# Rows turned on TensorE, and an angle's multiply-add moved to ScalarE, in the lead-in of a long-convolution kernel

## The chip, the cores and the metric

The kernel runs on one core of a Trainium2 chip. The time is device microseconds of one execution; the profile is one further execution, recorded by the hardware profiler. Engines are written as the profile writes them: PE (TensorE), DVE (VectorE), ACT (ScalarE), POOL (GpSimd), SP (SyncE, which issues most transfers).

## What is computed

Shapes: 2048 positions, 640 channels, MLP width 1728, all bfloat16. Cut to what matters here:

```python
mod = silu(c) @ w_mod                       # six vectors of 640: sa, ca, ga, sb, cb, gb
h = layernorm(x) * (1 + ca) + sa
# long convolution
k_shift = sum over t of k shifted by t * shift_k[:, t]     # 4 taps, per channel
kv = k_shift * v
y = irfft(rfft(kv, 4096) * rfft(ssm_k, 4096))[:2048] + kv * ssm_D
x = x + ga * (h * y)
h = layernorm(x) * (1 + cb) + sb
x = x + gb * mlp_block(h)                   # two GELU stages, four weight matrices
```

`ssm_D`, `c` and `shift_k` are small: 640, 640 and 640 x 4 numbers. Since y + kv * D is a convolution whose filter has D added to its first tap, the kernel adds D to column 0 of `ssm_k` before the transform.

## The kernel before

The FFTs are matrix products. Channels lie on 128 partitions in five blocks, b = 0 to 4. Each block of the filter is loaded (`sT`, a 512 KB transfer each), gets D added to its first column (L444), and is rearranged by a 32x32 transposition on DVE (L394, `to_slots`). Stage 1 of the transform (`stage1`) multiplies a block by the table F1bd: four matmuls of 256 columns (L407) per group, and one eviction of 1024 columns on ACT (L207) or DVE (L209). There are twenty such groups for the filter. Stage 2 (`stage2_half`, L427) needs all of them and a second table, `Gs` in region RG. Meanwhile the first blocks of k go through the shift filter (L463), a product with diagonal matrices made by L355 out of the shift coefficients.

All tables are computed in the kernel. An angle is an integer ramp (iota on POOL), multiplied by a per-partition number with an offset added, reduced modulo the table's length, and put through the ACT function Sin:

- F1bd: `angles` with 32 columns. DVE does the multiply-add (L292) and a bitwise AND (L293), twice each; ACT two sines (L321); POOL spreads the result into block-diagonal form (L332, L333).
- `Gs`, kb = 0, the first large table: the same with 512 columns, and a negated copy of the sines (L348, here on DVE).
- `Gs`, kb = 1: `angles_pool`, which reduces by rounding (L306 multiply-add, L308 rounding, L310 difference, each twice, on POOL, or DVE for one L306), then ACT sines (L316) and a negated copy on POOL (L348). The other half of RG is copied there by DMA (L353, L354).
- Later tables of 64 columns, and one in RK.

The per-partition numbers (`s32`, `s64`, `s32o`, `s64t`, `offc`) come from a block of small DVE instructions, L263 to L279, called the column setup below.

`Dcol`, `c_col` and `skT` hold D, c and the shift coefficients with the channel on the partition. Their transfers read one element of 2 bytes (8 bytes for shift_k) per partition and block: 640 pieces each. D is the first transfer on SP's queue, shift_k comes after four filter blocks, c much later (at 38.83 us).

Every piece of work is a task with a number, given to `add` in the order of the source. What runs where and in which order is written out by hand in a string, ORDER: `66D` is task 66 on DVE, `88P:0` is task 88 on PE with its PSUM result in slot 0 of four. A is ACT, G is POOL, S is SP. The engines take their tasks in the string's order and wait for each other by semaphores. The string begins

```python
0S 2S 19G 18D 50G 20D 21G 23D 22D 25A 4S 3S 1S 6S 27G 29D 36G 37G 28D 5S 8S 9S 11S 68G 10S
69D 24A 26G 88P:0 72G 73D 31A 30A 32D 38G 66D 89A 84P:1 85A 67D 90P:2 91A 86P:3 87D 39G 40A
```

0S is the load of D; 1S to 5S the filter blocks; 6S shift_k; 18D a few constants; 20D the column setup; 22D, 23D and 24A, 25A the F1 angles and sines; 26G F1bd; 28D to 31A the same for kb = 0 and 32D its negation; 68G, 72G and 66D the D additions of blocks 1, 3 and 0, and 69D, 73D and 67D their transpositions; 88P and 89A the first group of stage 1 with its eviction.

Of the kernel before, what the change touches and what calls it, by code (L numbers as in the profile page):

```python
# [8 lines left out]
BF = mybir.dt.bfloat16  # L9
F32 = mybir.dt.float32  # L10
I32 = mybir.dt.int32
ACT = mybir.ActivationFunctionType
# [14 lines left out]
0S 2S 19G 18D 50G 20D 21G 23D 22D 25A 4S 3S 1S 6S 27G 29D 36G 37G 28D 5S 8S 9S 11S 68G 10S 69D 24A 26G 88P:0 72G 73D 31A 30A 32D 38G 66D 89A 84P:1 85A  # L27
67D 90P:2 91A 86P:3 87D 39G 40A 102P:0 103A 100P:1 76P:2 70G 104P:0 41D 49G 101A 77A 42G 43G 105A 106P:3 107A 44A 45G 33S 47S 46S 71D 34S 12S 35S 48S
184S 181S 183S 182S 13S 14S 116P:1 92P:2 98P:0 74D 75D 117D 7S 99A 118P:3 119D 114P:0 15S 112P:1 113D 93A 110P:2 16S 115A 111A 96P:3 97A 94P:0 95D
82P:2 83A 80P:1 81A 78P:3 108P:0 51D 109A 52D 54A 56G 57D 53A 122P:2 79D 155P:1 156A 153P:0 154A 151P:3 152A 123D 157P:2 136D 120P:1 121D 173P:0 158A  # L30
55G 174A 171P:3 172A 177P:2 178D 175P:1 176A 161P:0 162D 141P:3 142A 167P:2 168D 147P:1 148A 58G 59G 163P:0 164D 165P:3 166A 137P:2 138A 145P:1 146A
230D 17S 149P:0 150A 190D 188D 126P:3 127D 139P:2 140A 60A 143P:1 199S 144A 124P:0 125D 179P:2 180A 187D 169P:3 170A 234P:1 235A 244P:2 159P:0 160A
128P:3 231D 242P:1 243A 245A 130P:0 61G 62G 186D 63G 64A 238P:1 239A 129D 131D 232D 248P:2 65G 196S 249A 246P:3 247A 185D 189G 191A 252P:0 202S 253A
134P:1 135D 132P:2 133D 236P:3 240P:1 237A 260P:0 261A 233D 250P:2 251A 241D 423D 200P:3 201A 258P:0 259D 319G 208S 192G 268P:2 269A 318S 197P:3 205S
198A 266P:1 267A 272P:2 273D 270P:3 271A 203P:0 284P:1 285A 292P:2 211S 204D 278P:3 279A 417D 276P:0 277A 342S 293D 426D 209P:1 210D 294P:2 295D 226S
290P:3 222G 291A 280P:1 281D 229G 227S 264P:0 274P:2 275D 343G 223G 265A 256P:3 262P:1 420D 206P:0 207D 257A 225G 254P:2 255D 282P:3 263A 286P:0
288P:1 287D 224G 312P:2 220S 283A 289A 212P:3 321D 320D 218G 213D 313A 328D 304P:0 305A 308P:1 316P:2 317A 217S 216G 302P:0 219S 214G 418D 228S 298P:2
215S 324P:3 325D 309A 221G 327G 326S 329D 322P:1 303A 336D 306P:0 299A 421D 323A 310P:2 296P:3 307A 334S 335G 337D 350S 297A 311A 300P:1 330P:0 301A
351G 332P:3 344D 345D 331A 314P:2 333A 315A 359G 340P:1 341A 338P:0 352D 348P:3 349A 353D 346P:2 358S 347A 360D 361D 354P:1 367G 339A 356P:3 368D 366S
369D 355A 364P:2 357A 375G 362P:0 376D 372P:1 374S 377D 401S 193A 363A 382S 370P:3 373A 384D 383G 385D 380P:0 378P:1 365A 392D 390S 391G 393D 422D  # L40
419D 424D 402P:2 427D 194D 403D 371A 388P:3 381A 379A 407S 389A 428D 386P:0 387A 416G 425D 396P:1 397A 394P:3 395A 398S 399P:0 400D 432P:12 429A 430D
434D 433A 489D 502A 510D 195G 413S 490D 491A 511D 530D 408P:3 513D 404S 405P:0 406A 531D 409A 512A 440S 492G 494D 475P:12 476A 477A 515D 532A 462P:03
463A 410S 411P:1 493G 495D 514G 435S 533D 534G 496A 497D 498G 441G 535D 464A 516D 536D 518D 499D 412A 517A 469P:20 537A 471A 519G 500P:3 538D 539G
414P:1 465G 470A 558D 449S 501D 520D 521P:3 436S 415A 507P:0 522A 443S 559D 560A 540D 541P:2 437S 542A 466P:13 431D 561D 562D 563A 564D 508A 546P:2
467D 468A 547A 548P:1 565G 448S 570D 528P:0 571D 566D 572D 567D 549A 573A 446S 568D 505P:3 506A 569A 574G 575G 447S 509G 529A 503D 523D 504D 621D 622D
472P:21 473A 526P:3 527A 623A 579D 580P:0 581A 576D 439S 543A 524D 577P:2 525D 624D 578D 625D 444S 438S 550P:3 627D 480S 551D 481S 626A 590P:0 591A
445S 482S 552A 588P:2 589A 595P:3 459D 628G 633D 629D 634D 553G 630D 631D 632A 635D 637D 636A 479S 554G 555D 556P:0 557A 592P:2 486S 596D 597A 638G
641A 639D 478S 488G 610P:3 612P:0 611A 593D 608P:2 606P:3 544D 594A 598D 613A 599G 474D 460A 603D 600D 601P:1 604P:0 609A 457D 607A 442S 454A 602A
640S 642S 651P:2 649P:3 461G 650A 450D 487S 652A 485S 605D 673P:0 667P:1 451D 545D 668A 674A 452G 582D 583D 484S 689D 690D 456A 458G 584D 585D 656P:3
692D 693D 653P:2 483S 614P:1 654D 655A 657D 694A 615D 659G 658A 671P:0 695D 660G 664D 665P:2 691A 661D 662P:3 663D 453D 669P:1 696G 701A 702D 703D  # L50
666A 735P:3 455G 672A 670A 697D 698D 699D 705G 737P:2 736A 739P:0 733P:1 616D 704A 643D 644D 645D 700A 738A 706G 709A 675P:32 710S 586D 587D 740A 755D
756D 757A 646A 707D 708S 758D 759D 717P:0 714D 761G 760A 762G 734A 763A 767D 777A 768D 711A 769D 719P:1 764D 780D 676P 718A 720A 721P:0 724P:1 647D
712D 765D 766A 677D 678D 770A 680S 771G 772G 683D 741P:32 648D 773D 774S 722D 775A 776S 785P:0 725D 726A 783P:1 713D 723A 824D 617S 825D 742P 821D
822D 827D 679S 681S 826A 743D 682S 727G 728G 731D 732S 823A 784A 828G 829A 786A 787P:3 729D 730S 833D 834D 835D 830D 831D 832A 837D 684D 685S 836A
620S 838G 790P:1 788D 789A 839D 840S 799P:0 791D 805P:3 806A 781D 841D 715D 716D 881D 749D 793G 792A 882D 842S 883A 803P:1 804A 794G 795A 796S 845P:2
846A 797D 778D 779D 884D 843P:3 844A 885D 887D 800A 801P:1 802A 618S 847P:2 848D 782D 941D 850P:3 851D 852A 886A 849A 619S 687S 798S 865P:0 866A
859P:1 860A 863P:2 807P:30 861P:1 744D 750D 753S 942D 944D 745S 853D 854G 855A 888G 893A 943A 752S 857A 889D 864A 945G 890D 856S 808P 858S 809D 891D
946A 947D 948D 950D 894D 862A 892A 895D 896A 897G 925P:2 926A 898G 751S 815D 747S 919P:3 901D 686S 920A 923P:1 899D 921P:0 949A 951G 922A 902S 900S
905P:2 906A 688S 903P:3 904A 952D 953S 956P:0 957A 954P:2 955A 907P:3 908D 910P:0 810D 958G 748S 959P:2 911D 913G 746S 816D 819S 924A 962P:1 867P:30
960D 817S 963D 813S 754S 912A 993P:2 909A 914G 812S 868P 915D 916S 917D 918S 977P:1 978A 994D 995A 996G 997G 971P:2 820S 972A 869D 998A 875D 927P:30  # L60
818S 964A 814S 811S 876D 961A 965D 966G 973P:1 967A 999S 969A 970S 870D 929D 974A 1028P:2 930D 975P:3 928P 968S 1000P:1 1001A 931S 935D 1002P:0 934S
976A 979P:13 981D 1003A 1006P:0 871S 873S 1004P:1 879S 1005A 872S 874S 936D 980P 987D 1029A 937S 933S 1026P:1 939S 1007A 877S 932S 988D 1024P:2 1025A
1032D 880S 878S 982D 983S 1008P:30 986S 991S 1027A 989S 1033D 1010D 938S 940S 1022P:2 1011D 1023A 1014S 1013S 1009P 1016D 984S 985S 1017D 1030P:13
1034D 992S 990S 1015S 1012S 1018S 1019S 1020S 1035D 1037S 1036S 1021S 1038S 1031P 1040D 1039S 1041D 1043A 1045A 1042S 1044S
# [72 lines left out]
def kernel(  # L137
# [51 lines left out]
    diagw = RQ[:, 0:2560].rearrange("p (b j m) -> p b j m", b=ND, j=4)  # L189
# [29 lines left out]
    c_col = mem.tile([P, ND], BF, name="c_col")  # L219
    skT = mem.tile([P, ND, 4], BF, name="skT")  # L220

    def ld_tiny(q, dst, src):
        with nc.allow_non_contiguous_dma(reason="tiny"):
            q.dma_start(dst, src)

    dma("SP", 8, lambda q: ld_tiny(q, Dcol[:], A_ssm_D.rearrange("(b p) -> p b", p=P)), w=[("Dcol", 0, 1)], rate=8.0)
    for b in range(ND):
        dma("SP", 512, lambda q, b=b: q.dma_start(sT[:, b, :], A_ssm_k[b * P:(b + 1) * P, :]), w=[("Ra", 2048 * b, 2048 * b + 2048)], rate=390.0)
    dma("SP", 8, lambda q: q.dma_start(skT[:], A_shift_k.rearrange("(b p) j -> p b j", p=P)), w=[("skT", 0, 1)], rate=30.0)
    dma("SP", 8, lambda q: ld_tiny(q, c_col[:], c.rearrange("o (b p) -> p (o b)", p=P)), w=[("ccol", 0, 1)], rate=12.0)  # L230
# [9 lines left out]
    b_neg = mem.tile([P, 1], F32, name="b_neg")  # L240
    stat = mem.tile([P, 3, 2, NT], F32, name="stat")
    s32 = mem.tile([P, 1], F32, name="s32")
    s32o = mem.tile([P, 1], F32, name="s32o")
    s64 = mem.tile([P, 1], F32, name="s64")
    s64t = mem.tile([P, 1], F32, name="s64t")
    pci = mem.tile([P, 2], I32, name="pci")
    offi = mem.tile([P, 2], F32, name="offi")
    offc = mem.tile([P, 6], F32, name="offc")

    def f(e):  # L250
        nc.vector.memset(mhalf[:], -0.5)
        nc.vector.memset(b_pos[:], PI_LO)
        nc.vector.memset(b_neg[:], -PI_LO)
        nc.vector.memset(stat[:], 0.0)
        nc.vector.memset(kT[:, :, 0:16], 0.0)
# [823 lines left out]
```

## Time and profile before

| | |
|---|---|
| median of three runs | 301.91 us (301.49 to 303.3) |
| span of the profiled execution | 298.7 us |
| PE busy | 269.7 us, 90% |
| DVE busy | 218.2 us, 73% |
| ACT busy | 208.3 us, 70% |
| POOL busy | 104.8 us, 35% |
| granted TensorE clock, mean | 0.975 |
| DVE busy from 26 to 40 us | 12.99 of 14.00 us |
| ACT busy from 26 to 40 us | 12.98 of 14.00 us |
| first block of the filter: issued, landed | 1.32, 5.40 us |
| load of D: issued, time to landing | 0.80, 3.0 us |
| load of shift_k: issued, time to landing | 3.29, 6.6 us |

The span runs from the first to the last instruction of one execution, so it is a little shorter than the time of a run. Busy shares are averages over stages that differ: what an instruction in the first 10 us is worth is read from what waits for it there. The lead-in before stage 1 and stage 1 itself take the first 26 us of the span.

### The profile page before, as it was taken

Reading aid. Unit: us, or ns where it says so; the run is one execution under the profiler, and the core shown is the slowest. Engines: PE = TensorE matmul, PEld = TensorE weight load, DVE = VectorE, ACT = ScalarE, POOL = GpSimd, SP = SyncE. Lnnn points to the kernel's source line nnn. Section 1 sums busy time; section 2 is a strip of 40 time slices with the busy share of each in tenths; the row PEclk is TensorE's granted clock in tenths of the full one; section 3 lists DMA queues with packets and bytes.
Section 4 is the critical chain, followed back from the end, with each engine's and each line's share of the span. In section 5 each row is a group of like instructions: output and inputs, shape, how many; then the busy total and the mean of one; then the engine's idle time right before and its main releaser. Section 6 shows DMA issues by size and latency. Waiting matters only on the chain.

```text
span 298.7 us, 7890 instructions
## 1 busy us (share of the span) xinstructions
PE 269.7 (90%) x3176; PEld 208.5 (70%) x3182; DVE 218.2 (73%) x438; ACT 208.3 (70%) x341; POOL 104.8 (35%) x237
## 2 busy tenths in 40 slices
PE   0999999999989766869999999999999999999993
PEld 0666755777878436648878677787788767887871
DVE  8998999999999998898759589886361544212442
ACT  4799989999999789979868775766854705431200
POOL 5864364453216591434275426120421321100000
PEclk9999999999999859799999999999999999999999
DMA  6999999898999920563700203223113030510112
GB/s 215 275 215 184 225 137 246 225 217 221 229 253 281 280 65 2 153 203 69 273 4 0 46 5 68 56 46 60 41 40 80 5 89 6 63 43 23 29 52 60
DMA packets 58356, 35.76 MB, mean 120 GB/s; under 512 B 40032, under 2 KB 55008, under 8 KB 58320
## 3 DMA queue, kind: packets, MB, share of 16 engines
q1 hardware_dynamic: 57136, 32.01, 46.3%
q0 software_dynamic: 1088, 3.21, 4.1%
q8 instruction: 25, 0.41, 0.6%
q14 instruction: 11, 0.09, 0.1%
q10 hardware_dynamic: 96, 0.04, 0.1%
HBM read 16.31 MB, written 2.62 MB: 63 GB/s over the span
## 4 chain that ended last, share of the span: by engine, by line
PE 51%; DVE 13%; ACT 11%; DMA 10%; POOL 6%; issue 5%; SPq 2%; DVEq 0%; POOLq 0%; ACTq 0%
PE ps_w L937 17%; PE ps_w L907 14%; ACT T L207 5%; DMA Ra<-in_A_q_dram 5%; PE ps_w L873 4%; PE ps_w L818 3%; PE ps_s L427 3%; ACT RG L729 3%; DVE Rb L617 3%; PE ps_ksh L463 2%; POOL lnv L715 2%; PE ps_s L407 2%; DMA RK<-R 2%; DVE R L756 2%; PE ps_mod L493 2%
## 5 line engine op out<-in xcount | busy, mean ns | idle before, releaser
L907 PE MATMUL ps_w<-R,T 128*128 128x256 bf16 (+1 forms) x630 | 63.8, 261 | 0.7 <-DMA R<-RH 0.7
L907 PEld LDWEIGHTS <-T 128*128 128x128 bf16 x630 | 55.5, 98 | 7.9 <-issue 2.0
L937 PE MATMUL ps_w<-T,R 128*128 128x320 bf16 x416 | 59.1, 299 | 0.0
L911 ACT ACTIVATE R<-ps_w 128x1024 bf16<-128x1024 f32 (+2 forms) x36 | 28.8, 827 | 41.9 <-PE ps_w L907 41.9
L937 PEld LDWEIGHTS <-R 128*128 128x128 bf16 x416 | 40.5, 98 | 15.2
L960 DVE TENSOR_TENSOR T<-ps_w,R 128x640 bf16<-128x640 f32 x15 | 12.3, 822 | 35.4 <-PE ps_w L928 18.1
L207 ACT CAST T<-ps_s 128x1024 bf16<-128x1024 f32 x32 | 30.4, 1029 | 3.2 <-PE ps_s L407 3.1
L207 ACT CAST R<-ps_s 128x960 bf16<-128x960 f32 (+1 forms) x35 | 30.8, 964 | 1.8 <-PE ps_s L427 1.6
L407 PE MATMUL ps_s<-F1bd,Rb 128*128 128x256 bf16 x160 | 23.3, 298 | 8.7 <-DVE Rb L394 8.1
L729 ACT ACTIVATE RG<-R 128x640 bf16<-128x640 bf16 x32 | 23.5, 734 | 9.9 <-DVE R L880 6.7
L407 PEld LDWEIGHTS <-Rb 128*128 128x128 bf16 x160 | 16.7, 107 | 14.7 <-DVE Rb L394 8.6
L873 PE MATMUL ps_w<-RG,R 128*128 128x320 bf16 x160 | 23.2, 299 | 2.1 <-ACT R L820 2.1
L715 POOL TENSOR_TENSOR lnv<-lnv,mhalf 128x2 f32<-128x2 f32 (+1 forms) x29 | 22.5, 775 | 2.3
L427 PE MATMUL ps_s<-T,RG 64*128 64x160 bf16 x512 | 21.2, 230 | 0.8 <-ACT R L207 0.6
L880 DVE SCALAR_TENSOR_TENSOR R<-ps_w,R 128x640 bf16<-128x640 f32 x16 | 12.9, 819 | 11.8 <-PE ps_w L873 11.6
L427 PEld LDWEIGHTS <-RG 64*128 64x128 bf16 x512 | 17.7, 94 | 5.1 <-issue 4.6
L818 PE MATMUL ps_w<-R,RG 128*128 128x256 bf16 (+1 forms) x200 | 20.0, 259 | 1.3 <-DMA R<-RK 0.6
L873 PEld LDWEIGHTS <-R 128*128 128x128 bf16 x160 | 15.4, 98 | 8.2 <-ACT R L820 2.4
L629 PE MATMUL ps_i<-EB,Rb 128*128 128x128 bf16 x160 | 19.0, 219 | 1.5 <-DVE Rb L617 1.4
L818 PEld LDWEIGHTS <-RG 128*128 128x128 bf16 x200 | 17.1, 102 | 3.5 <-issue 2.0
L628 PE MATMUL ps_i<-EA,Rb 128*128 128x128 bf16 x160 | 19.0, 219 | 0.4 <-ACT R L207 0.3
L714 POOL TENSOR_TENSOR lnv<-stat,lnv 128x2 f32<-128x2 f32 x19 | 4.0, 212 | 40.9 <-ACT RG L729 28.7
(178 smaller groups left out, 513.5 us busy)
## 6 DMA issues: line engine op xcount, KB each, us to landing
Ra<-in_A_ssm_k_dram SPq DMA_DIRECT2D x5, 512.0 KB, 5.7
R<-in_w_mod_dram SPq DMA_DIRECT2D x6, 400.0 KB, 6.0
out_dram<-RH SPq DMA_DIRECT2D x60, 40.0 KB, 1.6
T<-in_B_w_dram SPq DMA_DIRECT2D x5, 432.0 KB, 6.2
RH<-in_w_mod_dram SPq DMA_DIRECT2D x4, 400.0 KB, 4.4
Ra<-in_A_q_dram SPq DMA_DIRECT2D x4, 320.0 KB, 6.6
RK<-R SPq DMA_DIRECT2D x5, 256.0 KB, 4.5
RK<-R POOLq DMA_DIRECT2D x5, 256.0 KB, 5.3
```

Of the source, the lines that this page charges most:

```text
L207: nc.scalar.copy(dst, src(ps.tile))
L407: nc.tensor.matmul(psv[:, ml, :], lhsT=xL[:, s0:s0 + P], rhs=F1r, start=True, stop=True)
L427: nc.tensor.matmul(psv[:, g, j], lhsT=Gs[p, k, 64 - 64 * cc:192 - 64 * cc], rhs=T1h[h][p, cc * 32 + k], start=(cc == 0), stop=(cc == 1), t ...
L628: nc.tensor.matmul(psv[:, w, :], lhsT=Av[:, r_, :, g_], rhs=EAf, start=True, stop=False)
L629: nc.tensor.matmul(psv[:, w, :], lhsT=Bv[:, r_, :, g_], rhs=EBf, start=False, stop=True)
L715: nc.gpsimd.tensor_tensor(rs, rs, mhalf[:, 0:n], ALU.pow)
L729: add("ACT", 0.74, lambda e: nc.scalar.activation(junk, src, ACT.Square, scale=float(D) ** -0.5, accum_out=stat[:, li, 1, t:t + 1]), r=[sk ...
L818: nc.tensor.matmul(pt[:, fb, 0:cw], lhsT=w1_sb[:, b, 160 * fb:160 * fb + P], rhs=hT[:, b, 0:cw], start=(b == 0), stop=(b == ND - 1))
L873: nc.tensor.matmul(pt[:, hf, 0:320], lhsT=gsf[:, fb, c0:c0 + P], rhs=w2_sb[:, fb, 320 * hf:320 * hf + 320], start=(fb == 0), stop=(fb == 4))
L907: nc.tensor.matmul(pt[:, fl, 0:cw], lhsT=w3_sb[:, b, fb * P:(fb + 1) * P], rhs=xT[:, b, 0:cw], start=(b == 0), stop=(b == ND - 1))
L911: nc.scalar.activation(g3[g % 2][:, f0:f0 + fn, 0:cw], ps.tile[:, 0:fn, 0:cw], ACT.Gelu_apprx_tanh)
L937: nc.tensor.matmul(bank(i, hf), lhsT=gg[:, fb, i * P:(i + 1) * P], rhs=w4_sb[:, fb, 320 * hf:320 * hf + 320], start=(fb == 0 and i == 0), ...
```

## The change

It has four parts, all in the first 26 us.

1. D, c and shift_k are loaded as five rows (one per block of channels) into a corner of the region T01 that is not yet in use. A small mask, `eye`, made on POOL, and matmuls with five columns turn the rows into columns in PSUM, and ACT copies them to `Dcol` and to a new tile `csk`, which holds c and the shift coefficients. One matmul for D comes first on PE, five for c and shift_k come between the second and third group of stage 1. All three loads are now near the head of SP's queue. The diagonal matrices `diagw` change their order accordingly.
2. In the table kb = 0 the multiply-add is taken from DVE and given to ACT, as an Identity activation with scale and bias. The bitwise AND stays on DVE. The negated copy of that table goes from DVE to ACT.
3. The column setup is split: what the first tables need stays on DVE, and six instructions for the later tables go to POOL.
4. The D addition of block 1 goes from POOL to DVE, directly in front of its transposition.

From 26 us on, the order of the work is the one of before, with numbers higher by 8; only the c load is gone from there.

```diff
-0S 2S 19G 18D 50G 20D 21G 23D 22D 25A 4S 3S 1S 6S 27G 29D 36G 37G 28D 5S 8S 9S 11S 68G 10S 69D 24A 26G 88P:0 72G 73D 31A 30A 32D 38G 66D 89A 84P:1 85A
+0S 2S 19G 18D 27G 33G 22G 58G 44G 20D 36A 34A 29D 28D 21G 4S 6S 7S 3S 1S 5S 8S 9S 11S 10S 23P:3 24A 31A 30A 37D 35D 45G 76D 77D 32G 39A 38A 40A 96P:0
+80G 81D 46G 74D 97A 92P:1 25P:3 26A 93A 75D 98P:2 99A 94P:3 95D 47G 48A 110P:0 111A 108P:1 84P:2 78G 112P:0 49D 57G 109A 85A 50G 51G 113A 114P:3 115A
...
-    dma("SP", 8, lambda q: ld_tiny(q, Dcol[:], A_ssm_D.rearrange("(b p) -> p b", p=P)), w=[("Dcol", 0, 1)], rate=8.0)
+    csk = mem.tile([P, 5 * ND], BF, name="csk")
+    c_col, skT = csk[:, 0:ND], csk[:, ND:5 * ND].rearrange("p (j b) -> p b j", j=4)
+    rowD, rowc, rows = T01[0:ND, 0:P], T01[0:ND, P:2 * P], T01[0:ND, 2 * P:6 * P]
+    dma("SP", 8, lambda q: q.dma_start(rowD, A_ssm_D.rearrange("(b p) -> b p", p=P)), w=[("T01", 0, P)])
...
+    dma("SP", 8, lambda q: q.dma_start(rows, A_shift_k.rearrange("(b p) j -> b (p j)", p=P)), w=[("T01", 2 * P, 6 * P)])
+    dma("SP", 8, lambda q: q.dma_start(rowc, c.rearrange("o (b p) -> (o b) p", p=P)), w=[("T01", P, 2 * P)])
...
     def f(e):
+        nc.vector.tensor_single_scalar(pci[:, 1:2], pidx[:], 63, ALU.bitwise_and)
+        nc.vector.tensor_single_scalar(pci[:, 2:3], pidx[:], 64, ALU.bitwise_and)
         nc.vector.tensor_single_scalar(pci[:, 0:1], pidx[:], 31, ALU.bitwise_and)
+        nc.vector.tensor_single_scalar(pci[:, 3:4], pidx[:], 96, ALU.bitwise_and)
+        nc.vector.tensor_copy(s64[:], pci[:, 1:2])
+        nc.vector.tensor_copy(offi[:], pci[:, 2:4])
         nc.vector.tensor_copy(s32[:], pci[:, 0:1])
         nc.vector.tensor_scalar(offc[:, 0:1], offi[:, 0:1], s64[:], 0.5, ALU.mult, ALU.mult)
         nc.vector.tensor_scalar_add(offc[:, 1:2], offc[:, 0:1], 2048.0)
+    add("DVE", 1.3, f, r=[("pidx", 0, 1)], w=[("scol", 0, 1)])
+    def f(e):
+        nc.gpsimd.tensor_scalar(s64t[:], s64[:], 1.0 / 8192, None, ALU.mult)
+        nc.gpsimd.tensor_scalar(offc[:, 2:3], offi[:, 0:1], s64t[:], 0.5, ALU.mult, ALU.mult)
+        nc.gpsimd.tensor_scalar(offc[:, 3:4], offc[:, 2:3], 0.25, None, ALU.add)
+        nc.gpsimd.tensor_scalar(s32o[:], s32[:], 2.0 / 8192, 1.0 / 8192, ALU.mult, ALU.add)
+        nc.gpsimd.tensor_scalar(offc[:, 4:5], offi[:, 1:2], s32o[:], 0.5, ALU.mult, ALU.mult)
+        nc.gpsimd.tensor_scalar(offc[:, 5:6], offc[:, 4:5], 0.25, None, ALU.add)
+    add("POOL", 1.0, f, r=[("scol", 0, 1)], w=[("scolt", 0, 1)])
+    add("POOL", 0.2, lambda e: nc.gpsimd.affine_select(out=eye, in_=one.to_broadcast([P, ND]), pattern=[[-1, ND]],
+                                                       compare_op=ALU.is_equal, fill=0.0, base=0, channel_multiplier=1),
+        r=[("consts", 0, 1), ("T01", 6 * P + 16, 6 * P + 17)], w=[("T01", 6 * P, 6 * P + ND)])
+    def f(e):
+        pt = pst(psD, name="ps_row")
+        nc.tensor.matmul(pt[:, 0, 0:ND], lhsT=rowD, rhs=eye[0:ND, :], start=True, stop=True)
...
+    t1 = add("ACT", 0.2, lambda e: nc.scalar.copy(Dcol[:], psD.tile[:, 0, 0:ND]), w=[("Dcol", 0, 1)], use=psD)
...
+        nc.tensor.matmul(pt[:, 0, 0:ND], lhsT=rowc, rhs=eye[0:ND, :], start=True, stop=True)
+        for j in range(4):
+            nc.tensor.matmul(pt[:, 0, ND + ND * j:2 * ND + ND * j], lhsT=rows.rearrange("b (p j) -> b j p", j=4)[:, j, :], rhs=eye[0:ND, :], start=True, stop=True)
...
+    t1 = add("ACT", 0.2, lambda e: nc.scalar.copy(csk[:], psC.tile[:, 0, 0:5 * ND]), w=[("ccol", 0, 1), ("skT", 0, 1)], use=psC)
...
             def f(e, m_=m_, off=off):
-                nc.vector.tensor_scalar(m_, ti, s_col, off, ALU.mult, ALU.add)
+                if not split:
+                    nc.vector.tensor_scalar(m_, ti, s_col, off, ALU.mult, ALU.add)
                 nc.vector.tensor_single_scalar(m_, m_, q - 1, ALU.bitwise_and)
+            if split:
+                add("ACT", 0.25 + 0.00095 * n, lambda e, m_=m_, off=off: nc.scalar.activation(m_, ti, ACT.Identity, scale=s_col, bias=off),
+                    r=[keys[0], ("scol", 0, 1)], w=[k_])
...
+            if e == "ACT":
+                nc.scalar.mul(Gs[:, k2s, 128:192], Gs[:, k2s, 0:64], -1.0)
```

In the new string, 23P and 24A turn and copy D; 25P and 26A do it for c and shift_k; 36A and 34A are the two Identity passes and 37D and 35D the bitwise ANDs behind them; 31A and 30A the sines of F1bd and 32G F1bd; 40A the negation; 76D and 77D the D addition and transposition of block 1; 80G and 81D those of block 3; 96P and 97A the first group of stage 1.

## The prediction

> **What bounds the kernel now.** I read the page's forty slices first. PE, DVE and ACT are all near full from the second slice to the middle of the span, so a change in the lead-in counts only if it moves the start of the stage behind it. Then I read the chain of waits over the first 26 us (columns: start, length, what held the end):
>
> ```profile
> 0.80 0.46 SPq L224
> 1.32 4.08 DMA Ra<-in_A_ssm_k_dram
> 5.54 0.44 POOL Ra L444
> ...
> 10.66 2.41 POOL RQ L355
> 13.07 1.34 issue
> 14.46 1.95 POOL R L308
> 16.48 1.29 POOL R L310
> 17.80 0.63 ACT RG L316
> 18.43 7.31 ACT T L207 x8
> 25.79 1.83 PE ps_s L427 x44
> ```
>
> The chain starts at the filter's arrival (5.4), runs down POOL to the last sine of the second table (17.80), and from there is eight ACT evictions until stage 2 starts at 25.79. So 25.79 is the point that the change must move. The timeline of ACT says how tight the ACT side is (in brackets: idle time before, and what ended it):
>
> ```profile
> 0.79 1.28 ACT L321 ACT_TABLE_LOAD   x1 [0.79 <-PEq L1063]
> 4.13 0.32 ACT L321 ACTIVATE F1c<-R,b_neg 128x32 bf16<-128x32 int32 x1 [2.06 <-DVE R L293]
> ...
> 5.96 1.34 ACT L321 ACTIVATE RG<-R,b_pos 128x512 bf16<-128x512 int32 x2 [1.30 <-DVE R L293]
> 9.19 2.84 ACT L207 CAST T<-ps_s 128x1024 bf16<-128x1024 f32 x3 [1.89 <-PE ps_s L407]
> ...
> 17.80 0.63 ACT L316 ACTIVATE RG<-R 128x512 bf16<-128x512 f32 x1 [0.52 <-POOL R L310]
> ```
>
> From 9.19 on ACT has 0.52 us of idle time and no more; before 9.19 it has plenty, and its only table load sits at 0.79, where nothing waits for it. The timeline of DVE and PE shows what starts stage 1:
>
> ```profile
> 5.50 0.43 DVE L293 TENSOR_SCALAR R<-R 128x512 int32<-128x512 int32 x1
> 6.01 3.96 DVE L394 STREAM_TRANSPOSE Rb<-Ra 128x1024 int32<-128x1024 int32 x2
> 9.87 0.74 DVE L348 TENSOR_SCALAR RG<-RG 128x512 bf16<-128x512 bf16 x1
> 10.53 0.15 DVE L444 TENSOR_TENSOR Ra<-Ra,Dcol 128x1 bf16<-128x1 bf16 x1
> ...
> 8.12 6.95 PE L407 MATMUL ps_s<-F1bd,Rb 128*128 128x256 bf16 x36 [8.12 <-DVE Rb L394]
> ```
>
> PE starts at 8.12 when the first transposition ends; the table F1bd had been ready since 6.84 (POOL, L333).
>
> **What it takes away.** DVE loses seven tiny instructions of the column setup (L266, L268, L269, L275, L276, L278, L279; starts some 0.06 to 0.15 us apart, about 0.6), two L292 of 512 columns (0.54 each) and the negation L348 (0.74, or 0.66 by the next start); it gains one memset (0.03) and the D addition of block 1 (0.19): some 2.1 us net. SP keeps its 0.46 for the D load, and 640 two-byte packets become five rows; the c load leaves 38.83 (0.58 of SP) for the lead-in.
>
> **What it adds on ACT, step by step.** The compiled order of the changed kernel, readable without a run, shows what the diff doesn't: ACT now begins with a wait for the column setup, *then* a table load (a set with Identity), the two Identity passes, the copy of D, *a second table load* (the set with Sin), and only then the sines for F1bd. The old load was in front of every wait.
>
> 1. Column setup ends at 3.06 (L279: 2.91 + 0.15); less 0.6: 2.45.
> 2. First load, 1.28 by the row above: 2.48 to 3.76. Exposed, since it stands behind the wait.
> 3. Two Identity passes over 512 int32. Nearest row: the two L321 of 512, 1.34 for both. These have scale and bias as columns, so a little more: 1.4, to 5.18.
> 4. The copy of D, 128x5 out of PSUM: no such row. Between an accumulator read on ACT (0.19, L729) and a 128x32 ACTIVATE (0.32); 0.25, to 5.43. The row of D was issued at 0.80, as Dcol was, which landed in 3.0 (3.8), and its matmul is done by then.
> 5. Second load: 1.28, to 6.71. Both sines (4.13 to 4.66 before, 0.53): 7.25.
> 6. F1bd on POOL (5.93 to 6.84 before, 0.91) and two handoffs of 0.04: 8.2. PE starts at about 8.24, **0.12 later** than 8.12.
>
> Here a rule of the Trainium skill matters. The trace's other load is followed at once by the next instruction:
>
> ```profile
> 115.56 1.28 ACT L834 ACT_TABLE_LOAD   x1
> 116.85 1.10 ACT L834 ACTIVATE R<-ps_w1x 32x128 bf16<-32x128 f32 x4
> ```
>
> "ScalarE: Activation LUTs", section "What ACT_TABLE_LOAD costs", has the same 1283 ns but adds a drain of some 1380 ns to each switch, 2.66 us in all. At 115.56 there is none to be seen (116.84 to 116.85), so I take 1.28. By the page's sum the two loads would put PE's start at 8.24 + 2 x 1.38 = 11.0. The same page lists identity as a filler in every set, which would make one load enough; the compiled order has two, so that doesn't help.
>
> **DVE, with its stalls.** The four small F1 angle instructions (1.13 before) run 2.45 to 3.6. Each bitwise pass then waits for an Identity pass: 4.52 to 4.95, and 5.2 to 5.63. D addition at 5.65 (block 1 in SBUF at 5.40 before, not later now), transposition 5.85 to 7.85. The second transposition needs the D addition of block 3, which on POOL is queued behind F1bd: 8.2 + 0.19, so 8.4 to 10.4. DVE idles 0.55 there. It reaches the next D addition at 10.4 against 10.53: of 2.1 us saved, 0.1 is left.
>
> **POOL.** It gains six dependent 128x1 instructions and a small mask; small ones on POOL start some 0.3 apart (L559 51.20, L560 51.52), so about 2 us, from 2.5 to 4.5, with L306 (0.76) to 5.3. All that is hidden, as F1bd waits for the sines until 7.25. If the sines came earlier, it would show. After F1bd the rounding L308 starts 1.3 later than at 7.13, and the diagonal L355 ends at 14.45 and not 13.07. There POOL used to wait for DVE's L306 until 14.41, so the 1.34 us marked "issue" in the chain is used up: L308 at about 14.5, the last sine at about 17.85, 0.05 later. The diagonal needs c and shift rows: issued near 2.3 and 2.8; with skT's 6.6 from issue to landing they are there by 9.4 at worst, and PE reads them at about 10.1.
>
> **ACT behind 8.24.** The negation (0.65 like an L316) comes before PE's first group is done, 7.25 + 1.34 + 0.65 = 9.24 against 8.24 + 1.07 = 9.31: hidden by 0.07 only. Then the five row matmuls stand on PE between group 2 and 3. A matmul of this kernel costs between 0.04 (L427, 44 in 1.83) and 0.21 (L407, start to start); with five columns near the low end but a weight load each, 0.1: 0.5 in all, of which ACT waits about 0.3 after its first eviction; the copy is 0.25 more. So ACT is at 0.12 + 0.55 = 0.67 later, less its 0.52 of idle time: 17.95 at the last sine. That beats POOL's 17.85, so stage 2 starts **0.15 us later**, near 25.95.
>
> **Behind 26 us** both programs give the engines the same instructions in the same order. The c load leaves SP, and 1920 tiny packets shrink to 15; no wait of the chain is on them. One DVE wait of 0.38 at 25.88 is for a transfer and may go: bound -0.4 to 0, I take 0.
>
> Sum: the profiled execution 298.7 + 0.15 = 298.9; it lies 3.2 below the median 301.91, so about 302.1. A measurement of this kernel tells about 1% (3 us) from no change, and everything above fits well inside it.
>
> **Rivals.**
> *Faster.* The filter rows arrive earlier (the DMA rate was only 83 GB/s while the two-byte packets ran), and the first table load costs nothing on the path, for instance since ACT gets to it before the setup is finished. Then steps 2 to 6 are 1.25 earlier, PE starts when the first transposition ends, near 7.0, the second one follows without a stall, and stage 2 starts about 1.2 earlier: 300.7. For it: the old load ran at 0.79. Against it: the compiled order. Chance 0.15.
> *Slower.* The second load is longer than 1.28, as the page has it, so F1bd and with it both PE and the second transposition are late: 8.24 + 1.38 = 9.6. The idle time on ACT and POOL is already spent, so it reaches stage 2 in full: 0.15 + 1.38, 303.5. It decides as soon as PE's first stage-1 matmul is later than some 8.2. Drains at both loads would be 304.8. Chance 0.25, since 0.4 us of any kind on this ACT chain goes the same way.
> *Doing nothing* is my forecast: DVE's time is freed, but handed to waits. Chance 0.6, own range 301.4 to 302.8.
>
> **How the numbers follow.** The likeliest case gives 302.1. The range takes in 300.7 less 0.3 and 303.5 plus 0.5, for the scatter of the runs (301.49 to 303.3): 300.4 to 304.0. Over 1% slower needs 3 us: both drains and more, 0.06. Over 1% faster needs more than the faster case twice over, 0.05. Within 1%: 0.89.
>
> **What would show it.** Two table loads in ACT's timeline, the first near 2.5 and not 0.79, the second ending near 6.7; F1bd near 7.3 to 8.2; PE's first stage-1 matmul near 8.2, released by POOL and not by the transposition; a DVE gap of half a microsecond ahead of the second transposition; the last table sine near 17.9 with no idle ACT time before it; stage 2 near 25.9. I am wrong if PE starts before 7.6 or after 8.8, or if stage 2 starts with PE on time and yet half a microsecond off: then the row matmuls or the copies are mis-sized.

## The result

The changed kernel takes 303.35 us (median of 22 runs, 302.15 to 304.38) against 301.77 for the kernel before (22 runs beside it): ratio 1.0042, 95% interval 1.0025 to 1.006. Its profiled execution has a span of 301.6 us at a granted clock of 0.977, against 298.7 at 0.975. Executions fall into a faster and a slower state, and all times and ratios here are of the faster one. The forecast was 302.1 us and "no change"; 0.4 per cent was lost, and the place where it was lost is not the one that the forecast looked at.

First the lead-in, in the timeline of ACT of the changed kernel (start, length, line; in brackets the idle time before). Its line numbers differ from those of before by up to 32: L320 is the Identity passes, L349 the sines, L378 the negation, L208 the evictions, L344 the last table sine.

```profile
2.25 1.28 ACT L320 ACT_TABLE_LOAD   x1 [2.25 <-DVE offc L271]
3.54 1.52 ACT L320 ACTIVATE R<-R,offc,s 128x512 int32<-128x512 int32 x2
4.97 0.14 ACT L292 CAST Dcol<-ps_row 128x5 bf16<-128x5 f32 x1
5.13 1.28 ACT L349 ACT_TABLE_LOAD   x1
6.42 0.32 ACT L349 ACTIVATE F1c<-R,b_neg 128x32 bf16<-128x32 int32 x1
...
9.04 1.01 ACT L208 CAST T<-ps_s 128x1024 bf16<-128x1024 f32 x1 [0.34 <-PE ps_s L439]
10.13 0.18 ACT L302 CAST csk<-ps_row 128x25 bf16<-128x25 f32 x1
...
17.68 0.63 ACT L344 ACTIVATE RG<-R 128x512 bf16<-128x512 f32 x1 [0.43 <-POOL R L338]
```

Both table loads are there, both on the path, each 1.28 us, and the sine starts 0.01 us behind the second. Yet ACT still has 0.43 us of idle time ahead of the last sine. PE's and DVE's timelines show the handoff of F1bd and the stall of the second transposition:

```profile
7.99 1.22 PE L439 MATMUL ps_s<-F1bd,Rb 128*128 128x256 bf16 x5 [5.45 <-POOL F1bd L361]
```

```profile
8.13 2.07 DVE L426 STREAM_TRANSPOSE Rb<-Ra 128x1024 int32<-128x1024 int32 x1 [0.23 <-POOL Ra L476]
10.11 0.11 DVE L476 TENSOR_TENSOR Ra<-Ra,Dcol 128x1 bf16<-128x1 bf16 x1
```

The chain of waits from there (start, length, what held the end) has the shape of before's as far as the evictions:

```profile
14.33 1.96 POOL R L336
16.29 0.07 issue
16.36 1.30 POOL R L338
17.66 0.02 issue
17.68 0.63 ACT RG L344
18.31 3.65 ACT T L208 x4
```

Stage 2 in PE's timeline, before and changed:

```profile
25.79 1.83 PE L427 MATMUL ps_s<-T,RG 64*128 64x160 bf16 x44 [0.16 <-ACT T L207]
```

```profile
25.67 1.83 PE L459 MATMUL ps_s<-T,RG 64*128 64x160 bf16 x44
```

So the lead-in ends 0.12 us *earlier*, and the span is 2.9 us longer. To find where, I set every instruction behind it beside the same instruction of before. Up to 66 us the two keep within 0.1 us; about 0.6 is lost between 66 and 77, around the transfers RH<-RK and RK<-R; then nothing until 138; then it goes in steps: +1.2 at 138 to 142, +1.2 at 168 to 171, -0.5 at 200 to 207, +0.4 near 231. Some 1.4 of the 2.9 us is chance, though: the trace of before is 3.1 us shorter than its kernel's median time, and the trace of the changed kernel is 1.7 us shorter than its own.

The first step, in the chain of waits of before and then of the changed kernel, over the same 6 us:

```profile
138.73 0.70 POOL lnv L715
139.43 0.03 issue
139.45 0.81 DVE RH L724 x2
140.26 0.05 issue
140.31 0.73 PE ps_tr L772 x10
141.04 0.55 PE ps_w1x L828 x5
```

```profile
138.28 0.07 ACT RG L761
138.35 4.38 DMA R<-RK
142.73 0.14 issue
142.86 0.71 PE ps_w1x L860 x5
```

Before, the first layer's matmuls (ps_w1x) follow the layer norm's arithmetic. Afterwards PE stands idle for 1.1 us ahead of them, for a transposing transfer R<-RK that takes 4.4 us to land and not 2.6. The second step, in what the trace has on that transfer's issue line (durations in ns, min/median/max; 166 us before, 168 us after):

```profile
L765 SPq DMA_TRANSPOSE R<-RK x2: 1215/1218/1222, 166.6 to 167.9; - x2
```

```profile
L797 SPq DMA_TRANSPOSE R<-RK x2: 1217/1802/2388, 168.6 to 171.1; - x2
```

The first of two issues holds SP for 2.39 us and not 1.22, the second transfer starts 1.2 us later, and PE waits for it. Neither place has anything to do with D, c, the shift filter or the angles. What the change had moved there was the question for the experiments.

### The profile page after: what moved, and what is told of

It is laid out like the page before. It is cut to its first block, busy times and chain, and to the rows that moved or that the text cites. A ratio compares the mean times of both kernels' runs of the same rounds, so it can differ in the third digit from the quotient of the medians.

```text
span 301.6 us, 7914 instructions
## 1 busy us (share of the span) xinstructions
PE 270.1 (90%) x3188; PEld 207.5 (69%) x3188; DVE 216.5 (72%) x430; ACT 211.9 (70%) x347; POOL 105.5 (35%) x243
## 4 chain that ended last, share of the span: by engine, by line
PE 49%; DVE 18%; ACT 11%; DMA 7%; POOL 6%; issue 5%; SPq 1%; DVEq 0%; POOLq 0%; ACTq 0%
PE ps_w L969 16%; PE ps_w L939 13%; PE ps_w L905 4%; ACT T L208 4%; DVE Rb L649 4%; DMA R<-RK 4%; PE ps_s L459 3%; PE ps_ksh L495 3%; ACT RG L761 3%; PE ps_w L850 3%; PE ps_s L439 2%; POOL lnv L747 2%; DVE R L788 2%; DMA RK<-R 2%; DVE R L210 1%
## 5 line engine op out<-in xcount | busy, mean ns | idle before, releaser
L208 ACT CAST R<-ps_s 128x960 bf16<-128x960 f32 (+1 forms) x35 | 30.8, 965 | 2.0 <-PE ps_s L459 1.7
L208 ACT CAST T<-ps_s 128x1024 bf16<-128x1024 f32 x32 | 30.5, 1031 | 1.6 <-PE ps_s L439 1.5
L439 PE MATMUL ps_s<-F1bd,Rb 128*128 128x256 bf16 x160 | 22.3, 285 | 6.7 <-POOL F1bd L361 5.5
L439 PEld LDWEIGHTS <-Rb 128*128 128x128 bf16 x160 | 15.6, 101 | 12.4 <-DVE Rb L426 6.0
L495 PE MATMUL ps_ksh<-R,RQ 128*128 128x512 bf16 x80 | 18.8, 380 | 0.2 <-issue 0.2
```

What stands on the lines that cost most here:

```text
L208: nc.scalar.copy(dst, src(ps.tile))
L439: nc.tensor.matmul(psv[:, ml, :], lhsT=xL[:, s0:s0 + P], rhs=F1r, start=True, stop=True)
L495: nc.tensor.matmul(pt[:, i, :], lhsT=diagw[:, b, jj, :], rhs=kT[:, b, c0:c0 + 512], start=(jj == 0), stop=(jj == 3))
```

## The experiments

In the table, the columns on the right say how much later than in the trace of before the same instruction starts, at five marks on before's clock (a DVE scaling, and then four DVE additions behind matmuls). A rise from one column to the next is time lost in between. The ratio is to before in its own runs.

| kernel | ratio (95% interval) | span | 135.5 | 149.8 | 177.2 | 216.2 | 235.1 |
|---|---|---|---|---|---|---|---|
| changed | 1.0042 (1.0025 to 1.006) | 301.6 | +0.73 | +1.97 | +3.13 | +2.66 | +3.03 |
| changed, again | 1.0038 (1.0022 to 1.0054) | 301.7 | +0.46 | +1.55 | +2.57 | +2.10 | +3.08 |
| changed, c late | 1.0055 (1.0037 to 1.0073) | 301.6 | +0.69 | +1.71 | +2.71 | +2.23 | +3.01 |
| changed, sine first | 1.0020 (1.0003 to 1.0036) | 301.2 | +0.61 | +1.67 | +2.34 | +1.87 | +2.53 |
| before, c early | 1.0009 (0.9988 to 1.003) | 302.8 | +1.98 | +2.66 | +2.65 | +2.50 | +3.64 |
| before + 12 | 1.0048 (1.0024 to 1.0071) | 303.5 | +2.44 | +3.57 | +4.53 | +4.04 | +4.81 |
| before + 176 | 1.001 (0.9972 to 1.0047) | 304.4 | +5.42 | +6.25 | +6.22 | +5.73 | +5.73 |
| changed + 164 | 0.9995 (0.9972 to 1.0018) | 301.0 | +2.10 | +2.85 | +2.82 | +2.34 | +2.34 |
| changed + 244 | 1.0008 (0.9987 to 1.0029) | 301.7 | +1.42 | +2.16 | +2.13 | +2.22 | +3.05 |
| sine first + 164 | 0.9967 (0.9944 to 0.999) | 299.6 | +0.76 | +1.51 | +1.46 | +0.98 | +0.98 |
| the same, again | 0.9989 (0.9957 to 1.0021) | 299.5 | +0.62 | +1.45 | +1.41 | +0.92 | +0.93 |
| sine first + 244 | 1.0025 (1.0002 to 1.0049) | 301.4 | +2.35 | +2.34 | +2.30 | +2.44 | +2.44 |

Since the trace of before lies low among its own runs, the columns are read by their steps, and a version's worth by its ratio.

### First round: which part of the change?

**The changed kernel again**, unedited, to see whether the two steps come back.

> The changed kernel once more, as it is. In the profiles, stage 2 started 0.12 us earlier than before (25.67 against 25.79), yet the span ended 2.9 us later: the loss stands behind 66 us, at four transfers that landed late (the table copies RH<-RK and RK<-R, and two transpositions of xn at 138 and 168 us). If that is a property of the change, the same transfers are late again: stage 2 at 25.6 to 25.8, span 301 to 302, ratio to before 1.003 to 1.006. If it was the luck of one execution, stage 2 is the same, but the late transfers are others or none, the span is 299 to 301, and the ratio is then only as large as the mean of many such draws.

Both steps came back, with a ratio of 1.0038. They are the program's and not an accident of one execution. The loss between 66 and 77 us did not come back (0.1 there, and 0.5 near 40 instead).

**c as before.** The c load as 640 pieces at its old place behind the second value transposition, and its row matmul gone.

```diff
-    dma("SP", 8, lambda q: q.dma_start(rowc, c.rearrange("o (b p) -> (o b) p", p=P)), w=[("T01", P, 2 * P)])
+    dma("SP", 8, lambda q: ld_tiny(q, c_col, c.rearrange("o (b p) -> p (o b)", p=P)), w=[("ccol", 0, 1)])
...
-        nc.tensor.matmul(pt[:, 0, 0:ND], lhsT=rowc, rhs=eye[0:ND, :], start=True, stop=True)
...
```

> The changed kernel, but c is loaded as before (640 pieces of 2 bytes, into its own tile) at its old place on SP's queue, near 38 us; D and the shift filter stay rows. If the loss comes from c's load having left that place (SP issues the w_mod loads 1.8 us earlier, other transfers meet), it goes away: ratio to before 0.998 to 1.001. If not, 1.003 to 1.006 as for the changed kernel.

1.0055: the load is back at 38.7 and the loss stays. The moved c load is not the cause.

**Sine first.** A 128x1 sine put ahead of everything on ACT, so that the set with Sin is the one that gets loaded.

```diff
+    warm = mem.tile([P, 1], F32, name="warm")
...
+        nc.scalar.activation(warm[:], b_pos[:], ACT.Sin)
```

> The changed kernel plus one Sin activation of 128x1 on a constant ahead of everything on ACT, so that the set with Sin is loaded at 0.8 us, and Identity runs in it: one table load instead of two, and none on the path. My account of the lead-in: Identity at 2.3 as now less 1.28, the sines at 3.9 instead of 6.4, F1bd after POOL's small instructions at about 6.3, PE's first stage-1 matmul when the first transposition ends, 6.7 to 7.2 instead of 7.99, stage 2 at 24.4 to 25.0. Time 0.7 to 1.2 us less than the changed kernel, ratio to before near 1.001. Rival: the lead-in is hidden behind later waits; then stage 2 is earlier, but the time is that of the changed kernel, 1.004.

The Identity passes run in that set, so one load is left, in ACT's timeline at 0.79:

```profile
0.79 1.28 ACT L257 ACT_TABLE_LOAD   x1 [0.79 <-PEq L1097]
2.09 0.20 ACT L257 ACTIVATE warm<-b_pos 128x1 f32<-128x1 f32 x1
2.27 1.52 ACT L322 ACTIVATE R<-R,offc,s 128x512 int32<-128x512 int32 x2
3.69 0.14 ACT L294 CAST Dcol<-ps_row 128x5 bf16<-128x5 f32 x1
3.73 0.32 ACT L351 ACTIVATE F1c<-R,b_neg 128x32 bf16<-128x32 int32 x1
```

The sines start at 3.73 and not 6.42, 2.7 us earlier, and stage 2 starts at 25.37 in PE's timeline, 0.30 earlier than in the changed kernel (the 0.24 of a later expectation took 25.43 from the chain of waits). The expectation of 24.4 to 25.0 missed, and POOL's timeline says why:

```profile
6.80 0.19 POOL L478 TENSOR_TENSOR Ra<-Ra,Dcol 128x1 bf16<-128x1 bf16 x1 [0.50 <-DMA Ra<-in_A_ssm_k_dram]
...
14.04 1.94 POOL L338 TENSOR_SCALAR R<-R 128x512 f32<-128x512 f32 x1 [1.21 <-DVE R L336]
```

What comes next late is the filter's landing at 6.7, and then a multiply-add (L336) that DVE does at 13.40, no earlier than in the changed kernel (13.35), and for which POOL's rounding waits until 14.04. The two steps behind 135 us stay here too, so the second table load is not their cause.

**Before with c early.** The only edit is to the old kernel's c load, moved ahead of the later transposing loads.

```diff
-... 68G 10S 69D ...
+... 68G 10S 7S 69D ...
...
-... 117D 7S 99A ...
+... 117D 99A ...
```

> The kernel before, with only c's load (same 640 pieces) moved on SP's queue from 38.8 us to behind the first four transposing loads, near 18 us. If the absence of that load at 38.8 is what makes later transfers late, this alone costs 0.3 to 0.6%. If not, 0.999 to 1.001.

1.0009: nothing. Its profile has no step at 168 (+2.66 to +2.65). It does lose 0.7 at 134 to 137 and 1.1 near 231, and still its median time is that of before. So the steps at 140 and 231 are partly chance, in that the one trace of before has neither; the step at 168 is the one that tells the programs apart.

### Second round: the place of the instruction fetches

What every version with the steps has in common, and the two programs without them lack, are 12 more instructions on TensorE: the six row matmuls and their weight loads (10 where c isn't turned). The page lists a queue that brings them in:

```profile
q8 instruction: 25, 0.41, 0.6%
```

25 packets in 301.6 us, each of 16,384 bytes and some 0.9 to 1.4 us by the trace's records. In the trace of before there are, behind 185 us, 242 to 267 recorded TensorE instructions from one to the next, which is why I take the queue for TensorE's. (A second instruction queue, q14, has 11 packets of 8,192 bytes; in before, the changed kernel and before + 12 none of them falls at 136 to 145 or 165 to 175 us.) The Trainium skill, "Runtime: NRT & Kernel Launch", section "Instruction fetch mechanics", has blocks of 16 KiB, 256 instructions each, which fits, and calls the cost of crossing a block's border mostly hidden, which is what had to be tried. In the records, these are the starts on q8 between 123 and 240 us:

```text
before         129.3 143.5 154.5 171.8 185.0 200.8 215.8 230.9
changed        130.1 140.5 155.4 169.2 187.5 202.6 218.3 232.5
before + 12    131.3 142.2 157.5 170.7 188.9 203.9 219.6 234.7
changed + 164  123.9 135.6 149.7 162.0 176.1 193.7 209.9 223.0 237.0
changed + 244  131.3 146.4 156.7 174.0 186.8 202.9 217.9 233.1
before + 176   127.0 138.3 152.8 165.3 180.2 197.2 213.2 226.9
```

In the changed kernel the fetch at 140.5 falls between issue and landing of the R<-RK transfer of 138.35, and the one at 169.2 falls in the issue of 168.60 to 170.99. In before both come after the transfers. So the theory: the 12 instructions move the fetches into the transposing transfers, and that is the loss. It can be tried without anything else of the change.

**Before + 12 instructions.** Six 1x1 matmuls on TensorE in its idle time at 1.07 us, fed by a DVE memset.

```diff
+        nc.vector.memset(fone, 1.0)
...
+        pf = psA.tile([P, 2, 512], F32, name="ps_fill", tag="q3")
+        for _ in range(6):
+            nc.tensor.matmul(pf[0:1, 0, 0:1], lhsT=fone[0:1, :], rhs=fone[0:1, :], start=True, stop=True)
...
```

> The kernel before with six 1x1 matmuls (6 weight loads and 6 matmuls) put on TensorE in its idle time ahead of the first table; one DVE memset of a 128x1 column feeds them. No DMA, ScalarE or GpSimd instruction is touched. Theory (place of the instruction fetches): the 12 instructions move the fetches of 16 KB that follow TensorE's stream, so that those seen at 143.5 and 171.8 us come at about 140.5 and 168-169, inside the issue and landing of the transposing transfers: the pair of transposing issues at about 167-168 takes 3.2 to 3.7 us and not 2.54, the R<-RK transfer behind 138 lands in 3.4 us or more and not 2.6, the single issue at 200.5 goes from 1.69 to 1.20. Ratio to before 1.003 to 1.005, span 300.5 to 302. Rival (the loads as rows, ScalarE's table load or GpSimd's operations do it, or chance of the DMA queues): the 12 instructions do nothing, ratio 0.999 to 1.001, span within 0.7 of 298.7, and the pair at 167 stays at 2.54.

1.0048 (1.0024 to 1.0071): a loss as large as the change's, without the change. The DMA queues of its 138.5 to 142.5 us (packets, MB, share; then KB each, median us to landing) and the issue line at 170:

```profile
q8 instruction: 1, 0.02, 1.5%
...
T<-in_B_w_dram SPq DMA_DIRECT2D x1, 80.0 KB, 3.2
R<-RK SPq DMA_TRANSPOSE x2, 3.5
```

```profile
L770 SPq DMA_TRANSPOSE R<-RK x2: 1224/1710/2197, 170.2 to 172.5; - x2
```

A fetch is in the window, the 80 KB weight load lands in 3.2 us and not 2.3, and one issue takes 2.20 us. The 3.5 is the middle of two R<-RK transfers: the first landed in 2.7 us, the second in 4.3 (in before 2.7 and 2.6, in the changed kernel 2.7 and 4.4). The single issue at 205, which is the one at 200.5 in before, takes 1.20 us, as was expected. Its span, 303.5, is above what was expected: 2.4 us were lost before 135 us, a stretch in which the runs of the table differ by up to 2 us without an order.

**Changed + 164 instructions.** 82 such matmuls, 24 ahead of the D rows' matmul and 58 behind it, so that the fetches fall between the transfers.

```diff
...
+        for _ in range(58):
+            nc.tensor.matmul(pt[0:1, 1, 0:1], lhsT=one[0:1, :], rhs=one[0:1, :], start=True, stop=True)
```

> The changed kernel with 82 further 1x1 matmuls (164 TensorE instructions) in TensorE's idle time before 8 us, 24 ahead of the D rows' matmul and 58 behind it. Theory (place of the fetches): by the order of the instructions in the changed kernel's trace, the fetches then come at about 135, 145, 160, 174, 190, 206 and 221 us, outside the transposing transfers, so that the pair of issues at 168 takes 2.54 us again and those at 200 to 216 are freed too: ratio to before 0.998 to 1.001, span 298 to 299.5. If TensorE is still at the filling matmuls when the first table is ready (they would have to cost over 0.06 us each), all of it comes later by that much. Rival (the change itself makes the kernel longer behind 130 us): ratio 1.003 to 1.006, span 301 to 302.

0.9995 (0.9972 to 1.0018), apart from the changed kernel's 1.0025 to 1.006. The same two views, with no instruction fetch listed in 138.5 to 142.5:

```profile
T<-in_B_w_dram SPq DMA_DIRECT2D x1, 80.0 KB, 2.3
R<-RK SPq DMA_TRANSPOSE x2, 2.6
```

```profile
L802 SPq DMA_TRANSPOSE R<-RK x2: 1217/1223/1229, 169.5 to 170.8; - x2
```

The step at 168 is gone, the one at 140 is smaller (0.75, and it now arises at 134 to 137 on before's clock, at a DVE addition behind PE's matmuls, ahead of the transfer), and behind 149.8 nothing more is lost. Its span of 301.0 missed the 298 to 299.5 expected: 2.4 us went between 66 and 77. Fetches run there at 67.4 and 74.7 beside RH<-RK and RK<-R, but so they do at 65.2 and 72.4 in the changed kernel, which lost 0.6. The 82 matmuls took 2.3 us of idle time, and PE's first stage-1 matmul stayed at 8.00.

**Changed + 244 instructions.** With the change's 12 that makes 256, one block, so the later fetches should fall where before's fall.

> The changed kernel with 122 of the 1x1 matmuls (24 ahead of the D rows' matmul, 98 behind it; about 3.2 us of TensorE's idle time). The 12 instructions that the change adds and these 244 make 256, which is one fetch of 16 KB, so that the later fetches fall where those of the kernel before fall. Theory (place of the fetches): the pattern of before comes back in every mark: fetches at about 143.5 and 171.8 us and none in 138 to 142, the pair of issues at 167 at 2.54 us, the single issue at 200.5 at 1.5 to 1.7 and not 1.20, and between 135 us and the end 0.0 to 0.3 us more than before. Ratio 0.998 to 1.001. Rival (any longer head of TensorE's program helps, by clock or by time, without regard to the place): the pattern is that of the changed kernel with 164 more, 1.20 at 200.5, with fetches at 135 and 162.

They do: 146.4 and 174.0 are 144.2 and 171.9 on before's clock. The mark of before's place of fetches is the single issue at 200.5 (before), which takes longer there than in the changed kernel. SP's timeline of before, of the changed kernel and of this one:

```profile
200.53 1.69 SPq L765 DMA_TRANSPOSE R<-RH  x1
```

```profile
203.67 1.20 SPq L797 DMA_TRANSPOSE R<-RH  x1
```

```profile
202.68 1.77 SPq L802 DMA_TRANSPOSE R<-RH  x1
```

The collision at 200 is back and the one at 168 is gone. Ratio 1.0008 (0.9987 to 1.0029); the interval overlaps a little with the changed kernel's, so here the places decide more than the time. So it isn't just a longer head of the program that helps: adding 256 instructions in all brings before's places back. That 1.69 also explains the half microsecond that the changed kernel won back at 200 to 207. Between 135 and 235 this run lost 1.6 all the same, and the expectation of 0.0 to 0.3 missed: 0.74 at 134 to 137, as with 164, and 0.83 near 231 (fetch at 233.1), where before's own fetch at 230.9 is at the same place in the program and was not seen to cost anything.

All thirteen traces agree on the issues. Each has 22 transposing issues from SBUF to SBUF. In 13 of these 286 a fetch started between 0.03 us before the issue's start and 0.58 behind it, and they took 1.36 to 2.39 us; the other 273 took 1.20 to 1.29, also where a fetch was ending or where one started over 0.8 us into the issue.

**Before + 176** was to show the same on the old kernel, with 88 matmuls.

> The kernel before with 88 such matmuls (176 instructions), so that its TensorE stream is as long as that of the changed kernel with 164 more and its fetches fall at the same places. Theory: it has no collision at 140 and 168 and loses none of the two that before has at 200 and 216: ratio to before 0.997 to 1.000, and within 0.001 of the changed kernel with 164 more: the change itself is worth nothing in either direction. Rival (the change itself costs 1.3 us): this one stays at 0.999 to 1.001 and the changed kernel with 164 more lies 0.003 to 0.006 above it.

1.001 (0.9972 to 1.0047): too scattered to tell (10 runs, 300.45 to 304.8). Its trace is that of a run of 306.1 us outside these, and only places and steps are read from it. No fetch falls into a transposing issue, the pair takes 2.54 us and the single issue 1.20, and from 135.5 us on its steps are +0.83, -0.03, -0.49 and 0.00: those of the changed kernel with 164 (+0.75, -0.03, -0.48, 0.00), in a program without the change.

**Sine first + 164 and + 244**, to see whether one table load and a good place of the fetches together beat both kernels.

> The changed kernel with the 128x1 sine ahead of everything on ScalarE (one table load) and with the same 164 TensorE instructions. Theory: the 0.24 us that the single table load gained at the start of stage 2 now stays: ratio to before 0.997 to 1.000, span 297.8 to 299.2, 0.0 to 0.3 us below the changed kernel with 164 more. Rival: as with the other, ratio 1.001 to 1.004, as it was without the filling.

> The changed kernel with the 128x1 sine first and 164 TensorE instructions, once more, with more rounds, since it was the only one below before (0.9967, 0.9944 to 0.999) and its neighbour with 244 was above it (1.0025) by a later first 20 us. Theory (place of the fetches, here at 10.6, 133.6, 160.6 us and so on): the pair of issues at 168 at 2.54, the single one at 202 at 1.20, stage 2 at 25 us or before, ratio 0.995 to 0.999. Rival (chance of the runs): ratio 0.999 to 1.002.

> The changed kernel with the 128x1 sine first and the same 244 TensorE instructions. Theory: marks as in the changed kernel with 244 more, less the 0.2 us at the start of stage 2: ratio to before 0.997 to 1.000. Rival: ratio as without the filling, 1.001 to 1.003.

The first gave 0.9967 (0.9944 to 0.999), and its second try 0.9989 (0.9957 to 1.0021), with spans of 299.6 and 299.5 that have neither the step at 168 nor the one near 231. Stage 2 starts at 25.16 and 25.24; the first span and the second start are 0.4 and 0.2 us later than was expected. It is the best version seen, but a gain over before isn't shown by both tries. With 244 it was 1.0025 (1.0002 to 1.0049), a miss: its profile loses almost nothing behind 135 us (0.1), as expected, but 2.2 before 26 us. DVE's D addition waits there for the filter, and the TensorE program has a fetch at 7.0 us, while the filter is being loaded:

```profile
10.15 2.43 DVE L483 TENSOR_TENSOR Ra<-Ra,Dcol 128x1 bf16<-128x1 bf16 x1 [0.70 <-DMA Ra<-in_A_ssm_k_dram]
```

With 164 the first fetch is at 10.6, and the same addition takes 0.30. One pair of traces doesn't show that the fetch makes it so, but there are more: in all three traces with a fetch at 6.8 to 7.1 us (this one, changed + 244 and before + 176) the third filter block landed at 9.0 to 9.6 us, and in the ten others at 7.9 to 8.5.

## Why the prediction held in its verdict and failed in its cause

The time of 303.35 lies in the range of 300.4 to 304.0 by luck: the range reached so high for a longer second table load, which did not occur. Step by step, from the traces:

| term of the prediction | predicted | measured |
|---|---|---|
| column setup ends | 2.45 | 2.17 |
| first table load, exposed | 2.48 to 3.76 | 2.25 to 3.53 |
| two Identity passes | 1.4 | 1.52, overlapping the copy by 0.09 |
| copy of D | 0.25 | 0.14 |
| second table load, no drain | 1.28, to 6.71 | 1.28, to 6.41 |
| PE's first stage-1 matmul | 8.24 | 7.99 |
| DVE's gap before the second transposition | 0.55 | 0.23 |
| row matmuls, copy of csk | 0.5 and 0.25 | 0.3 and 0.18 |
| POOL's rounding L308 (now L336); last table sine | 14.5; 17.85 on POOL, 17.95 on ACT | 14.33; 17.68, with 0.43 of ACT idle |
| start of stage 2 against before | +0.15 | -0.12 |
| all behind 26 us | 0 | the loss |

**The lead-in was right in the main**: two loads on the path, POOL and not the transposition as PE's releaser, the second transposition stalled by POOL's D addition, and DVE's freed 2 us handed to waits. Most sizes were a little high (the Identity passes were low), and together they are 0.27 us. One path was wrong: ACT's idle time was to be used up, so that ACT and not POOL would set the start of the last sine (17.95 against 17.85); it kept 0.43 us, and POOL set it, at 17.68. Of the sizes the setup matters most: 0.28 early, and it carries through to PE's start at 0.25 early.

**The rule against the row.** With a drain of 1.38 us at each load, as weighed from the Trainium skill, "ScalarE: Activation LUTs", section "What ACT_TABLE_LOAD costs", PE would by that estimate have started near 11.0. It started at 7.99; the row at 115.56 was the better guide.

**The failed step** is the sentence that behind 26 us both programs give the engines the same instructions in the same order, and the 0 taken for it with a bound from -0.4 to 0. Measured are 3.0 us behind 26 us in the two traces, of which some 1.4 is chance, and 1.6 between the medians. The instructions are the same. What isn't is their position in TensorE's stream: the change's 12 instructions on PE move each border of 256 instructions, and with it a 16 KB fetch, against everything that comes after. Twelve instructions alone, without the change, gave 1.0048 (1.0024 to 1.0071), and the change with its stream filled up gave 0.9995 and 1.0008. The step that goes with the fetch in every trace is the one at 168: 0.7 to 1.2 us in the five traces with a fetch in that pair of issues, none in the seven other edited ones. The bound was on the wrong side as well: I asked only what the shorter loads could free, and not what the added instructions could disturb.

**The rivals.** The faster one wanted the first load off the path and had 1.2 us for it. Sine first takes it off, and stage 2 moves by 0.30: the filter's landing and DVE's multiply-add come next. The filter did arrive earlier in the changed kernel, its first block at 4.61 us and not 5.40, but its D addition, at 5.66, wasn't waiting for it. The slower one, a longer second load, did not occur; the number that it gave, 303.5, is near the measured 303.35 for another reason.

**What stays open.** In all profiles that I compared, the pair of issues at 166 to 170 took 3.2 to 3.7 us where a fetch started inside it (five runs) and 2.53 to 2.55 where none did, and the single issue at 200 took 1.5 to 1.8 with a fetch and 1.20 without. Why an issue on SP is held up by a fetch for TensorE isn't shown. How much of the step at 140 is the fetch's is open: the five traces with a fetch beside R<-RK lose 1.0 to 1.2 us there, but six of the seven other edited ones lose 0.7 to 0.8 at 134 to 137 instead. Nor is it shown why there is a loss near 134 and 231 in some executions and none in others, nor how much of the loss between 66 and 77 us, which varies from nothing to 2.4 us, is due to fetches. The fetches moved by some 3 us at 140 and 168 for 12 instructions; the likely reason is that the border now lies ahead of the matmul that waits for the transfer instead of behind it, but that was only argued.

## What to carry to other kernels

An edit at the head of a program shifts the instruction stream for the rest of it. Where a result differs from the sum of the edited stage, set the two traces side by side instruction by instruction, and when the steps lie where nothing was edited, look at the fetches of the busiest engine against the short transfers that the path waits for, and try the unedited kernel with the same number of idle instructions added. Effects of this size belong to where the program happens to lie: a half per cent from a small edit isn't yet the edit's own worth.

## What was not expected of the hardware

- A 16 KB fetch for TensorE during the issue of a 128-row transposing transfer went with an SP issue time of 1.93 to 2.39 us at 168 where it is 1.22 without one, and of 1.53 to 1.81 at 200 where it is 1.20; with a fetch beside the second R<-RK of 138, that transfer landed in 4.2 to 4.4 us and not 2.6.
- TensorE ran long rows of 1x1 matmuls at 26 to 27 ns a pair of weight load and matmul (88 in 2.33 us, 98 in 2.58; 24 took 0.74), so a stream can be lengthened by 244 instructions in 3.3 us of idle time.
